# Another beginning for block 0, the next block's elimination and part of the activation on VectorE, and later stores

## The chip, the cores and the metric

The kernel runs on one core of a Trainium2 chip. Its engines have queues of their own: TensorE (PE; PEld is its weight load), VectorE (DVE), ScalarE (ACT), GpSimd (POOL), and SyncE (SP), which here issues all the DMAs. Each engine works through its queue in order and waits on semaphores for the others. The metric is the device time of one execution in microseconds: 2344.46 us is the median of three runs (2343.63 to 2352.79).

## The reference

Three stages follow each other. Shapes: batch 4, heads 8, sequence 768, head size 48; 3072 tokens of 384 columns; a hidden layer of 2048; 8 experts with 1024 hidden columns each.

```
k_n = k / (norm(k) + 1e-6)
for t in range(768):                       # delta rule, one state per (batch, head)
    y[t]  = q[t] @ state
    state = state + beta[t] * outer(k_n[t], v[t] - state.T @ k_n[t])
x = y as (tokens, 384)
h = x @ w_in                               # 384 -> 2048
g = h * tanh(softplus(h))                  # "Mish"
x = g @ w_out                              # 2048 -> 384
P = exp(x @ w_gate - max)                  # (3072, 8)
8 times: P /= row sums; P /= column sums; P *= 3072 / 8
out = sum over e of P[:, e] * (relu(x @ w1[e]) @ w2[e])
```

All inputs are fp32, except that w_in and w_out reach the kernel as 64-bit words whose bits it turns into fp32 itself.

## The kernel before

**Blocks.** The sequence is cut into six blocks of 128 steps (two chunks of 64), so a block has 512 tokens. The main loop goes through the blocks. In one block it does the hidden layer of 2048 in 16 units (`s0` to `s15`, then four marks `f1` to `f4` without a first product), and then expert 0 in 8 units (`s16` to `s23`). A unit is 128 hidden columns: nine products into a PSUM bank of 512 columns (`gemm1`, L296), the activation, and the second product. Each fp32 operand is split into a rounded high part and a remainder (`xh`, `xl`; `gh`, `gl`; two halves of `w`), and three products are added up. After the loop the experts 1 to 7 are done by another code, which the change does not touch.

**The delta rule of the next block** is laid beside a block's units. For each block, `st_g` multiplies keys with keys and queries, VectorE masks the results (`gx`), two or three transpositions bring them into `lane`, and 30 pairs of small operations (`elim_ops`, L784 and L790) invert the triangular diagonal blocks: a product, then an addition, each waiting for the one before. `st_lane_out` transposes back into `t11` and `yd`. `st_m1` and `st_m2` join the half blocks by products (copies at L815 and L607), `st_place` puts the diagonal blocks back. Then a chain of 16 stages follows, four kinds (`st_z`, `st_w`, `st_s`, `st_y`) for two chunks and two batch pairs, each reading what the one before wrote through VectorE.

`window(c)` says at which mark of block c each step stands: `PLACES` gives per block the mark of `st_lane_out`, the marks of the chain, of the square sums, mask products, `st_g`, operand loads and the start of the elimination. Elimination steps wait in a list `eq`, from which `fill(us)` and `tick` (after each VectorE operation made through `vec`) take as many as their costs allow.

**Block 0** has nothing in front of it, so its own delta rule is the beginning of the kernel: loads, `st_gk` and norms, elimination, joining, chain, transposition into `x1h`, `x1l` (`st_x1`), then the first unit. In it TensorE is given fillers: `warm(n)` is n products of 512 zero columns into a spare bank, and `run_warm(cols, ...)` puts some behind each stage. During the beginning and block 0 the weights are also decoded: `begin_decode` scales the high words on ScalarE (L202), three VectorE operations (L185, L188, L193) put the words together, and `convert` rounds the high part on ScalarE (L248), subtracts on GpSimd (L249), and stores the result in DRAM (`wd`, L253), so that later blocks load it with one DMA (L242). The buffers of the words are reused, so that a decode four chunks on waits for a conversion; some are the key and query tiles of block 0.

The activation of block 0 is `m_a` (Mish from PSUM into `mi_x` in SBUF), `m_c` (copy to `gh`, L977, and the remainder `gl` on GpSimd, L978). `y0_done` and `x2_done` copy results into `xr` and issue its store right there (L959, L1002). In the last block `g_load` prepares the next experts' weights and at once fetches the following ones.

Of the kernel before, what the change touches and what calls it, by code (L numbers as in the profile page):

```python
# [84 lines left out]
def delta_mish_sinkhorn_kernel(  # L85
# [144 lines left out]

    def convert():
# [190 lines left out]
    def g_load():  # L422
# [19 lines left out]
        g_fetch()  # L442
# [84 lines left out]
    if True:  # L527
# [173 lines left out]


# [18 lines left out]
        def st_gq(c, t):  # L721
# [46 lines left out]
        def lane_in_ops(c):  # L768
# [5 lines left out]
            )  # L774

# [89 lines left out]
        def first_r(c, t):  # L865
            rt[c, t] = r_p.tile([128, DM], F32, tag="r", name="r")
            nc.scalar.activation(out=rt[c, t], in_=vt(c)[:, t, :], func=AF.Copy, scale=-1.0)
# [75 lines left out]
        y0ps = {}  # L943

# [7 lines left out]
        def y0_done(c):  # L952
# [6 lines left out]
            nc.sync.dma_start(out=y0_dram[c], in_=y)  # L959
# [10 lines left out]
        def m_a(u):  # L970
            nc.scalar.activation(out=mi_x[u % 2], in_=hps.pop(u), func=AF.Mish)

        def m_c(u):
            p = mi_x[u % 2]
# [3 lines left out]
            nc.gpsimd.tensor_tensor(out=l, in0=p, in1=h.bitcast(F32), op=ALU.subtract)  # L978
# [14 lines left out]
        def x2_done(c):  # L993
# [8 lines left out]
            nc.sync.dma_start(out=x2_dram[c], in_=xr)  # L1002
# [31 lines left out]
        with tc.manual_schedule():  # L1034
# [8 lines left out]
            for t in range(4):  # L1043
                load_part(0, t, 1)
            for t in range(4):
                load_kq(1, t)
            load_vt(0)
            for n in range(4):
                fetch(n)
            load_vt(1)  # L1050
            nc.sync.dma_start(out=id_sb, in_=ident)
# [19 lines left out]
            for op in root_ops(0) + norm_ops(0, ALL):  # L1071
                op()
            for t in range(4):
                prep_mb(0, t, (nc.vector, nc.gpsimd)[t % 2])
                g0[t]()
            for _, op in lane_in_ops(0):
                op()
# [5 lines left out]

            for t in range(4):
                prep_ss(1, t)
            prep_root(1)
            nc.scalar.activation(out=mi_s[0][:, 0:1], in_=seed_sb, func=AF.Mish)
# [4 lines left out]
            el(12)  # L1092
            for op in root_ops(1) + norm_ops(1, ALL):
                el(1)
                op()
            for t in range(4):
                prep_mb(1, t, nc.gpsimd)
            for t in range(2):
                mask_p(0, t)
            for t in range(2):  # L1100
                prep_v(0, t)
                first_r(0, t)
            for t in range(4):
                mask_g(1, t, nc.gpsimd)
            for t in range(2, 4):
                prep_v(0, t)
                mask_p(0, t)
            for n in range(3):
                begin_decode(n)
            el(len(e0) - 16)  # L1110
# [4 lines left out]
            in1 = deque(op for _, op in lane_in_ops(1))  # L1115
            in1.popleft()()
            elim_eng = [nc.gpsimd]
            ops1 = deque(op for _, op in elim_ops(1, elim_eng))

            def elim1(n, eng):  # L1120
                elim_eng[0] = eng
                for _ in range(min(n, len(ops1))):
                    ops1.popleft()()

            run_warm(2048, lambda: st_m1(0, 0), lambda: st_m1(0, 1))
            st_place(0, 0, (0, 2))
            while in1:
                in1.popleft()()
            run_warm(2048, lambda: st_m2(0, 0))

            def step(pool, decode, make, dve):
                elim1(pool, nc.gpsimd)
                decodes(decode)
                elim1(dve, nc.vector)
                converts(make)

            step(8, 1, 0, 0)
            run_warm(1536, lambda: st_w(0, 0), lambda: st_w(0, 1))
            st_place(0, 1, (0, 2))
            run_warm(1280, lambda: st_m2(0, 1))  # L1140
            step(8, 2, 1, 0)
            run_warm(1024, lambda: st_s(0, 0), lambda: st_s(0, 1))
            run_warm(1024, lambda: st_y(0, 0), lambda: st_y(0, 1))
            for n in range(4, 6):
                fetch(n)
            begin_decode(3)
            step(4, 3, 2, 0)
            run_warm(1024, lambda: st_z(0, 2), lambda: st_z(0, 3))
            step(4, 4, 2, 8)
            run_warm(512, lambda: st_w(0, 2), lambda: st_w(0, 3))  # L1150
            begins(6)
            step(2, 5, 3, 0)
            run_warm(512, lambda: st_y(0, 2), lambda: st_y(0, 3))
            for n in range(6, 8):
                fetch(n)
            step(4, 6, 5, 6)
            converts(4)
# [17 lines left out]
        def drain_decode():  # L1175
            decodes(U1)
            converts(U1)

        PLACES = [
            (5, spread(5 + 3, 26, 2, 16), 21 - 5,  # L1180
             [21 - 2, 21 - 1, 21, 21 + 1], spread(21, 27, 2, 8), 18, 26, 24),
            (3, spread(3 + 3, 19, 1, 16), 8 - 5,
             [8 - 2, 8 - 1, 8 + 1, 8 + 3], spread(8, 19, 1, 8), 1, 27, 19),
# [284 lines left out]
```

## Time and profile before

| what | value |
|---|---|
| median of three runs | 2344.46 us |
| profiled execution | 2351.13 us, span 2349.4 us |
| TensorE busy | 2262.2 us, 96% of the span |
| VectorE, ScalarE, GpSimd busy | 1239.3, 619.7, 527.3 us |
| mean granted TensorE clock | 0.968 of full speed |
| first product of a unit (L296) | 864 of 419 ns and 432 of 409 ns |
| elimination of block 0 ends, first unit starts, block 1 starts | 59.9, 111.5, 275.4 us |
| block 2, 3, 4, 5 start; end of the loop | 428.6, 570.4, 711.6, 838.1, about 954 us |

A granted clock of 1.00 is 2.4 GHz and 0.50 is 1.2 GHz; between them stands a mean over a stretch. The page's slices show VectorE at eight to nine tenths only in the first 180 us, and TensorE near nine tenths behind that. A row of the profile names a line, an engine, an operation, the written and read tiles and their shapes.

### The profile page before, as it was taken

To read this page: it belongs to the slowest core of one execution; us is meant where nothing else is said; L and a number is where in the kernel's file an instruction comes from. 1 tells how busy PE (TensorE), PEld (TensorE's weight loads), DVE (VectorE), ACT (ScalarE), POOL (GpSimd) and SP (SyncE) were. 2 spreads that over 40 slices of the span, in tenths; PEclk is the share of its full clock that TensorE was granted. 3 is DMA by queue.
4 is the path that set the end of the run, shared out by engine and by line. 5 is a ranking of instruction groups with operands and counts; after the bars stand their busy time and mean duration, and the time that the engine had idled before them with its cause. 6 is when DMAs were issued, how large, how long until landed. Compare 5 with 4: busy or idle time off the path is not lost.

```text
span 2349.4 us, 41970 instructions
## 1 busy us (share of the span) xinstructions
PE 2262.2 (96%) x18012; PEld 2090.3 (89%) x18012; DVE 1239.3 (53%) x2009; ACT 619.7 (26%) x1012; POOL 527.3 (22%) x439
## 2 busy tenths in 40 slices
PE   8688999999999999999999999999999999999998
PEld 4477777878788887899999999999999999999998
DVE  8884724518153112776554555555555555545554
ACT  5244332333223233222211221131122122112111
POOL 5586442241411133131300110030020002002000
PEclk6799989999999999999999999999999999999999
DMA  6357643636444455432332132231223113221321
GB/s 174 122 202 214 200 151 127 213 122 202 158 158 162 162 215 215 166 119 93 122 135 81 55 121 81 82 127 49 81 81 135 65 71 121 81 81 68 108 87 48
DMA packets 74441, 297.04 MB, mean 126 GB/s; under 512 B 7504, under 2 KB 39504, under 8 KB 68880
## 3 DMA queue, kind: packets, MB, share of 16 engines
q1 hardware_dynamic: 74256, 294.36, 36.3%
q8 instruction: 142, 2.33, 0.4%
q14 instruction: 43, 0.35, 0.0%
HBM read 247.15 MB, written 47.19 MB: 125 GB/s over the span
## 4 chain that ended last, share of the span: by engine, by line
PE 51%; issue 30%; DVE 7%; DMA 5%; POOL 5%; SPq 1%; ACT 1%; POOLq 0%; DVEq 0%; ACTq 0%
PE psh L296 12%; PE o L1347 11%; PE b L487 10%; PE x L989 8%; PE y L318 3%; DMA gr<-in_w_dram 3%; POOL gw L439 2%; DVE t L784 1%; DVE lane L790 1%; DMA w<-wd 1%; POOL gx L439 1%; PE psa L739 1%; PE psa L878 1%; PE psa L912 1%; DVE lane L772 1%
## 5 line engine op out<-in xcount | busy, mean ns | idle before, releaser
L487 PE MATMUL b<-gx,gw 128*128 128x256 f32 x3564 | 448.7, 283 | 6.4 <-DVE gate L363 2.5
L487 PEld LDWEIGHTS b<-gx,gw 128*128 128x128 f32 x3564 | 441.3, 191 | 10.1 <-ACT gt L509 3.7
L1347 PE MATMUL o<-gw,gh 128*128 128x384 f32 x1728 | 440.4, 335 | 2.0 <-DVE acc L1352 2.0
L514 ACT ACTIVATE gh<-gt 128x1024 fp32r<-128x1024 f32 x168 | 178.3, 1061 | 620.3 <-DVE gt L513 620.3
L296 PE MATMUL psh<-xh,w 128*128 128x512 f32 x864 | 291.4, 419 | 20.8 <-DMA w<-wd 11.6
L1347 PEld LDWEIGHTS o<-gw,gh 128*128 128x128 f32 x1728 | 307.6, 189 | 2.5 <-issue 2.5
L515 DVE SCALAR_TENSOR_TENSOR gl<-gt,gh 128x1024 fp32r<-128x1024 f32 x168 | 207.7, 1236 | 189.4 <-ACT gh L514 189.4
L1347 PE MATMUL o<-gw,gl 128*128 128x384 f32 x864 | 289.7, 335 | 0.0
L510 DVE TENSOR_TENSOR gt<-b,gt 128x512 f32<-128x512 f32 x168 | 116.2, 691 | 309.6 <-PE b L487 245.3
L1347 PE MATMUL o<-gx,gh 128*128 128x384 f32 x960 | 247.5, 339 | 2.4 <-DVE acc L1352 2.4
L487 PE MATMUL b<-gx,gx 128*128 128x256 f32 x1980 | 244.3, 280 | 2.0 <-ACT gt L509 1.0
L487 PEld LDWEIGHTS b<-gx,gx 128*128 128x128 f32 x1980 | 240.5, 188 | 3.8 <-ACT gt L509 1.7
L978 POOL TENSOR_TENSOR gl<-x,gh 128x512 fp32r<-128x512 f32 x96 | 128.0, 1333 | 405.7 <-ACT gh L977 397.2
L439 POOL TENSOR_TENSOR gw<-gr,gw 128x512 fp32r<-128x512 f32 x72 | 90.8, 1294 | 567.5 <-ACT gw L437 567.5
L296 PEld LDWEIGHTS psh<-xh,w 128*128 128x128 f32 x864 | 162.1, 197 | 62.6 <-issue 17.1
L296 PE MATMUL psh<-xl,w 128*128 128x512 f32 x432 | 176.6, 409 | 3.9 <-DVE xl L607 3.9
L1347 PEld LDWEIGHTS o<-gx,gh 128*128 128x128 f32 x960 | 171.6, 188 | 2.9 <-issue 2.0
L1347 PEld LDWEIGHTS o<-gw,gl 128*128 128x128 f32 x864 | 162.4, 188 | 0.4
L1347 PE MATMUL o<-gx,gl 128*128 128x384 f32 x480 | 162.6, 339 | 0.0
L509 ACT ACTIVATE gt<-b 128x256 f32<-128x256 f32 x168 | 63.8, 380 | 349.8 <-PE b L487 328.9
L989 PE MATMUL x<-gh,w 128*128 128x512 f32 x576 | 151.4, 399 | 0.0
L439 POOL TENSOR_TENSOR gx<-gr,gx 128x512 fp32r<-128x512 f32 x40 | 51.3, 1312 | 436.0 <-ACT gx L437 436.0
(182 smaller groups left out, 3026.0 us busy)
## 6 DMA issues: line engine op xcount, KB each, us to landing
w<-wd SPq DMA_DIRECT2D x120, 768.0 KB, 4.5
gx<-xcd SPq DMA_DIRECT2D x36, 2304.0 KB, 9.0
gr<-in_w_dram SPq DMA_DIRECT2D x56, 384.0 KB, 3.7
wd<-w SPq DMA_DIRECT2D x24, 768.0 KB, 4.4
xcd<-gx SPq DMA_DIRECT2D x6, 2304.0 KB, 11.6
kq<-in_qkb_dram SPq DMA_DIRECT2D x20, 256.0 KB, 6.7
vt<-in_vtok_dram SPq DMA_DIRECT2D x6, 768.0 KB, 8.6
kq<-in_w_in_dram SPq DMA_DIRECT2D x12, 384.0 KB, 4.6
```

Source lines behind the costliest of these rows:

```text
L296: mm(ps, lhsT=wi(u, pw, kc), rhs=(xh, xl)[px][:, kc, :], start=(n == 0), stop=(n == 3 * KD - 1))
L318: mm(o[t], lhsT=(h, l)[ph][:, t * 128:(t + 1) * 128], rhs=wo(u, pw, 0, DM), start=(f == 0 and n == 0), stop=(f == U2 - 1 and n == 2))
L439: nc.gpsimd.tensor_tensor(out=w[:, 1, q:q + 512], in0=r[:, q:q + 512], in1=w[:, 0, q:q + 512].bitcast(F32), op=ALU.subtract)
L487: mm(ps, lhsT=w[:, pw, a * 128:a * 128 + 128], rhs=x[:, px, b, :], start=(n == 0), stop=(n == last))
L509: nc.scalar.activation(out=t[:, 7], in_=b0[:, 0], func=AF.Copy)
L510: tt(out=t[:, 0:7:6], in0=b1, in1=t[:, 7:8].to_broadcast([128, 2, 256]), op=ALU.add)
L514: nc.scalar.activation(out=h, in_=t[:, 0:4], func=AF.Relu)
L515: nc.vector.scalar_tensor_tensor(out=l, in0=t[:, 0:4], scalar=0.0, in1=h.bitcast(F32), op0=ALU.max, op1=ALU.subtract)
L739: mm(ps[0:64, :, i], lhsT=k[64:64 + D, 0, h, :], rhs=k[64:64 + D, 0:2, h, :], start=True, stop=True)
L978: nc.gpsimd.tensor_tensor(out=l, in0=p, in1=h.bitcast(F32), op=ALU.subtract)
L989: mm(x2ps[c][k], lhsT=wo(u, pw, k * 128, k * 128 + 128), rhs=(h, l)[pg], start=(f == 0 and n == 0), stop=(f == U1 - 1 and n == 2))
L1347: mm(o[t], lhsT=(h, l)[ph][:, z, (t % 2) * 128:(t % 2) * 128 + 128], rhs=w[:, pw, at:at + DM], start=(g == 0 and fi == 0 and n == 0), stop ...
```

## The change

**The beginning.** `diag_left` copies, on ScalarE, the second diagonal block of each product beside the first, so that `lane_in_one` needs one transposition; GpSimd clears the copies behind it. The scalings of v in block 0 go to ScalarE (`prep_v_act`, and `first_r` with the scale `minus_ne`). The products with the queries stay in four PSUM banks, and VectorE masks them later, between the chain's results. The mask products and maskings of block 1 come after block 0's elimination instead of beside it. The load of v of block 0 goes ahead of block 1's operands. `run_warm` becomes `run`, with single fillers left. The decode scalings of four chunks stand behind ScalarE's copies of products; four chunks are converted before the loop, the fifth is only begun.

**Block 0.** Mish is written in place into its PSUM bank for the 16 units, and VectorE computes the remainder. Of block 1's elimination GpSimd does 18 steps, VectorE takes the others from `eq`, three or so per unit (`fill(1.2)`). `PLACES` puts block 1's `st_lane_out` at mark 11 instead of 5, and its chain two by two at marks 14 to 22 instead of 8 to 15; the products for block 2 stand two marks later, the loads of their operands where they stood.

**Stores.** The store of a converted chunk is issued after the next conversion's fetch, the stores of `xr` at unit 4 and at the third unit of expert 0. In the last block a fetch for expert 1 stands two marks behind the `g_load` that frees its buffer.

```diff
+    late_stores = deque()
+    def flush_stores():
+        while late_stores:
+            late_stores.popleft()()
...
         if kind(i) == "again":
+            flush_stores()
             nc.sync.dma_start(out=w.bitcast(F32), in_=w_dram[ch])
...
-        if ch in w_dram:
-            nc.sync.dma_start(out=w_dram[ch], in_=w.bitcast(F32))
...
+        flush_stores()
+        if ch in w_dram:
+            late_stores.append(lambda: nc.sync.dma_start(out=w_dram[ch], in_=w.bitcast(F32)))
...
             def post():
-                raw(k[0:64, 1], ps[0:64])
-                raw(k[64:128, 2], ps[64:128])
+                for p, o in ((0, k[0:64, 1]), (64, k[64:128, 2])):
+                    if masked:
+                        nc.vector.tensor_tensor(
+                            out=o, in0=ps[p:p + 64],
+                            in1=mask_sb[p:p + 64, None, :].to_broadcast([64, H, CH]), op=ALU.mult,
+                        )
+                    else:
+                        raw(o, ps[p:p + 64])
...
+        def diag_left(c, t):
+            g = gx(c)[:, t]
+            for p in (32, 96):
+                nc.scalar.activation(out=g[p:p + 32, :, 0:32], in_=g[p:p + 32, :, 32:64], func=AF.Copy)
+        def lane_in_one(c):
+            v = gx(c).rearrange("p t h x -> p x (t h)")
+            return [
+                (1.94, lambda: nc.vector.transpose(out=lane, in_=v[:, 0:32, :])),
...
         def m_a(u):
-            nc.scalar.activation(out=mi_x[u % 2], in_=hps.pop(u), func=AF.Mish)
+            if u < U1:
+                nc.scalar.activation(out=hps[u], in_=hps[u], func=AF.Mish)
...
         def m_c(u):
-            p = mi_x[u % 2]
+            p = hps.pop(u) if u < U1 else mi_x[u % 2]
...
-            nc.gpsimd.tensor_tensor(out=l, in0=p, in1=h.bitcast(F32), op=ALU.subtract)
+            eng = nc.vector if u < U1 else nc.gpsimd
+            eng.tensor_tensor(out=l, in0=p, in1=h.bitcast(F32), op=ALU.subtract)
...
-            nc.sync.dma_start(out=y0_dram[c], in_=y)
+            late_xr.append(lambda: nc.sync.dma_start(out=y0_dram[c], in_=y))
...
-            run_warm(1024, *[lambda t=t: st_gq(0, t) for t in range(3)])
-            run_warm(1024, lambda: st_gq(0, 3))
+            gq = [st_gq(0, t, True) for t in range(4)]
             for t in range(4):
-                run_warm(512, *[lambda hf=hf: st_g(1, t, hf, False) for hf in range(2)])
...
-            (5, spread(5 + 3, 26, 2, 16), 21 - 5,
...
+            (11, two(14, 15, 17, 18, 19, 20, 21, 22), 16, [21, 22, 23, 24], two(23, 24, 25, 26), 18, 26, 26),
...
-                    if not c and f < m0:
-                        elim1(10, nc.gpsimd)
+                    if f == 4:
+                        flush_xr()
...
-                    fill(2.0)
+                    fill(2.0 if c else 1.2)
...
+                    if f == U1 + 2:
+                        flush_xr()
```

**Three places in the queues.** In the rows below, `bits` and `kq` are words being decoded, `lane` and `t` belong to the elimination, `us` to the chain, `xl` and `gl` are remainders, `psa` and `psh` are PSUM banks.

VectorE before, where the first unit's operands are made (the last elimination steps of the beginning, the low parts `xl`, chain results):

```order
L784 TENSOR_TENSOR t_169<-lane 128x198 [waits DVE_49]
L790 TENSOR_TENSOR lane<-lane,t_169 128x9x22 [waits DVE_49]
L607 TENSOR_TENSOR xl_1208<-psa,xh_1207 128x512 [waits Activation_49] x3
L607 TENSOR_TENSOR us_164<-psa,us_165 48x384 [waits PE_49]
L607 TENSOR_TENSOR us_164<-psa,us_165 48x384
L607 TENSOR_TENSOR us_166<-psa,us_167 48x384 [waits PE_49]
L607 TENSOR_TENSOR us_166<-psa,us_167 48x384
```

VectorE after, at the same place:

```order
L185 TENSOR_SCALAR bits_177<-bits_177 128x768 [waits DMAHW7_49,DMAHW6_49]
L188 SCALAR_TENSOR_TENSOR bits_177<-bits_177 128x768 [waits DVE_49]
L193 SCALAR_TENSOR_TENSOR bits_177<-bits_177 128x768 [waits DVE_49]
L824 TENSOR_TENSOR t_169<-lane 128x210 [waits Pool_49]
L830 TENSOR_TENSOR lane<-lane,t_169 128x21x10 [waits DVE_49]
L824 TENSOR_TENSOR t_169<-lane 128x220 [waits DVE_49]
L617 TENSOR_TENSOR xl_1152<-psa,xh_1151 128x512 [waits Activation_49] x3
L1031 TENSOR_TENSOR gl<-psh,gh 128x512 [waits Activation_49]
```

Ahead of `xl` three elimination steps now stand whose first waits for GpSimd, and the first remainder `gl` of block 0 comes behind it.

VectorE before, in the middle of block 0's units (decode steps and the joining of block 1):

```order
L185 TENSOR_SCALAR kq_142<-kq_142 128x768 [waits DMAHW7_49,DMAHW0_49]
L188 SCALAR_TENSOR_TENSOR kq_142<-kq_142 128x768 [waits DVE_49,Activation_49]
L193 SCALAR_TENSOR_TENSOR kq_142<-kq_142 128x768 [waits DVE_49]
L607 COPY mb_179<-psa 32x512 [waits PE_49]
L607 COPY mb_179<-psa 32x512
L185 TENSOR_SCALAR kq_143<-kq_143 128x768 [waits DMAHW5_49,DMAHW4_49,Pool_49]
L188 SCALAR_TENSOR_TENSOR kq_143<-kq_143 128x768 [waits DVE_49,Activation_49]
L193 SCALAR_TENSOR_TENSOR kq_143<-kq_143 128x768 [waits DVE_49]
```

VectorE after, in the middle of block 0's units:

```order
L1031 TENSOR_TENSOR gl<-psh,gh 128x512 [waits PE_49,Activation_49]
L824 TENSOR_TENSOR t_169<-lane 128x228
L830 TENSOR_TENSOR lane<-lane,t_169 128x12x19 [waits DVE_49]
L824 TENSOR_TENSOR t_169<-lane 128x220 [waits DVE_49]
L185 TENSOR_SCALAR kq_145<-kq_145 128x768 [waits DMAHW5_49,DMAHW4_49]
L188 SCALAR_TENSOR_TENSOR kq_145<-kq_145 128x768 [waits DVE_49]
L193 SCALAR_TENSOR_TENSOR kq_145<-kq_145 128x768 [waits DVE_49]
L1031 TENSOR_TENSOR gl<-psh,gh 128x512 [waits PE_49,Activation_49]
```

Between two remainders there are now three or four elimination steps and one decode; the joining has moved to later units.

SyncE before, at the end of block 0 and the start of block 1 (weight loads `w`, the store `y0d`, the operands `kq`):

```order
L242 DMA w_88<-wd_93 128x1536 [waits DMAHW3_49,PE_49]
L959 DMA y0d_73<-xr 128x1536 [waits DMAHW4_49,DVE_49,Activation_49]
L617 DMA kq_146<-in_qka_dram 48x1024 [waits DMAHW5_49]
L618 DMA kq_146<-in_qkb_dram 64x2x512 [waits DMAHW6_49]
L617 DMA kq_147<-in_qka_dram 48x1024 [waits DMAHW7_49]
L618 DMA kq_147<-in_qkb_dram 64x2x512 [waits DMAHW0_49]
L617 DMA kq_148<-in_qka_dram 48x1024 [waits DMAHW1_49]
L618 DMA kq_148<-in_qkb_dram 64x2x512 [waits DMAHW2_49]
L617 DMA kq_149<-in_qka_dram 48x1024 [waits DMAHW3_49]
L618 DMA kq_149<-in_qkb_dram 64x2x512 [waits DMAHW4_49]
L242 DMA w_89<-wd_94 128x1536 [waits DMAHW5_49,PE_49]
L242 DMA w_1209<-wd_95 128x1536 [waits DMAHW6_49,PE_49]
```

SyncE after, at the same place, from the last operands on:

```order
L628 DMA kq_148<-in_qkb_dram 64x2x512 [waits DMAHW1_49]
L627 DMA kq_149<-in_qka_dram 48x1024 [waits DMAHW2_49]
L628 DMA kq_149<-in_qkb_dram 64x2x512 [waits DMAHW3_49]
L250 DMA w_89<-wd_94 128x1536 [waits DMAHW4_49,PE_49]
L250 DMA w_1153<-wd_95 128x1536 [waits DMAHW5_49,PE_49]
L250 DMA w_85<-wd_96 128x1536 [waits DMAHW6_49,PE_49]
L1008 DMA y0d_73<-xr 128x1536 [waits DMAHW7_49,DVE_49,Activation_49]
L250 DMA w_86<-wd_97 128x1536 [waits DMAHW0_49,PE_49]
```

The store stands behind three more weight loads; the operands of block 3 still stand ahead of these.

## Rows read from the trace of the kernel before

**Rows 1.** Windows: stretch, length, busy time (instructions) per engine, granted clock, DMA share, GB/s.

```profile
0.00:111.45 111.45, 85.04 (x1125) 54.89 (x1125) 96.90 (x149) 44.26 (x133) 61.95 (x66) 0.69 0.46 141
122.24:202.78 80.54, 73.69 (x934) 60.63 (x930) 67.41 (x61) 39.80 (x58) 64.02 (x44) 0.96 0.61 206
202.78:275.44 72.66, 64.77 (x443) 55.18 (x439) 33.50 (x70) 25.25 (x48) 40.45 (x35) 0.91 0.70 222
838.06:954.40 116.34, 110.91 (x503) 92.66 (x502) 33.80 (x80) 38.69 (x60) 41.04 (x31) 0.96 0.52 192
```

**Rows 2.** TensorE waits, start: who for whom, total us, times, longest.

```profile
PE psa L826 <- DVE t L799: 7.1, 1, 7.1
PE psa L912 <- DVE us L607: 6.5, 1, 6.5
PE psh L296 <- DVE xl L607: 3.9, 1, 3.9
```

**Rows 3.** VectorE timeline: start, us, engine, line, operation, tiles, shapes, idle before.

```profile
17.35 3.89 DVE L772 STREAM_TRANSPOSE lane<-gx 32x1024 f32<-32x1024 f32 x2
37.44 1.35 DVE L784 TENSOR_TENSOR t<-lane 128x240 f32<-128x240 f32 x1
59.89 2.01 DVE L799 STREAM_TRANSPOSE t<-lane 128x1024 f32<-128x1024 f32 x1
75.78 0.96 DVE L193 SCALAR_TENSOR_TENSOR xr<-xr 128x768 int32<-128x768 int32 x1
```

**Rows 4.** VectorE groups, 260 to 290 us: count, busy us, mean ns, idle before.

```profile
L790 DVE TENSOR_TENSOR lane<-lane,t 128x30 f32<-128x30 f32 (+14 forms) x30 | 11.6, 387 | 0.8
L784 DVE TENSOR_TENSOR t<-lane 128x30 f32<-128x30 f32 (+14 forms) x30 | 11.5, 382 | 0.9
L311 DVE SCALAR_TENSOR_TENSOR hl<-psh,hh 128x512 fp32r<-128x512 f32 x4 | 2.7, 682 | 0.0
```

**Rows 5.** Windows: products with fillers; block 0’s elimination beside GpSimd.

```profile
16.75:48.00 31.25, 31.25 (x272) 21.24 (x272) 29.96 (x54) 21.15 (x98) 15.86 (x14) 0.50 0.73 219
28.40:44.90 16.50, 16.50 (x119) 11.62 (x118) 16.02 (x15) 8.15 (x22) 15.83 (x13) 0.50 0.74 264
```

**Rows 6.** TensorE groups, 57 to 111 us: fillers between the joining stages.

```profile
L1022 PE MATMUL spare<-f 128*128 128x512 f16 (+1 forms) x41 | 14.9, 468 | 0.0
```

**Rows 7.** GpSimd groups, 73 to 98 us: elimination of block 1.

```profile
L790 POOL TENSOR_TENSOR lane<-lane,t 128x30 f32<-128x30 f32 (+11 forms) x12 | 8.9, 738 | 0.9
```

**Rows 8.** TensorE groups, 428 to 571 us: one chain operation.

```profile
L878 PE MATMUL psa<-r,gx 64*64 64x48 f32 x128 | 4.5, 220 | 0.0
```

**Rows 9.** VectorE groups, 117 to 200 us: decoding in block 0.

```profile
L193 DVE SCALAR_TENSOR_TENSOR kq<-kq 128x768 int32<-128x768 int32 x10 | 17.8, 1782 | 0.3
L188 DVE SCALAR_TENSOR_TENSOR kq<-kq 128x768 int32<-128x768 int32 x10 | 16.4, 1640 | 3.7 <-ACT kq L202 2.8
L185 DVE TENSOR_SCALAR kq<-kq 128x768 int32<-128x768 int32 x10 | 10.3, 1027 | 0.1
```

**Rows 10.** GpSimd groups, 117 to 200 us: the activation’s remainder.

```profile
L978 POOL TENSOR_TENSOR gl<-x,gh 128x512 fp32r<-128x512 f32 x13 | 20.9, 1608 | 3.2 <-ACT gh L977 2.5 <-DMA wd<-w 0.6
```

**Rows 11.** TensorE waits in block 0 after its first unit.

```profile
PE psa L739 <- issue: 5.5, 1, 5.5
```

**Rows 12.** TensorE waits in block 1, and clock behind the wait.

```profile
PE psh L296 <- DMA w<-wd: 6.7, 1, 6.7
290.00:310.00 20.00, 13.27 (x151) 10.62 (x151) 8.53 (x12) 5.34 (x11) 7.83 (x3) 0.57 0.63 200
```

**Rows 13.** SyncE timeline, beginning of block 1.

```profile
281.85 0.32 SPq L959 DMA_DIRECT2D y0d<-xr  x1
287.39 3.72 SPq L242 DMA_DIRECT2D w<-wd  x4
```

**Rows 14.** TensorE waits in blocks 2 and 3.

```profile
PE psa L861 <- issue: 2.7, 1, 2.7
```

**Rows 15.** TensorE waits in blocks 4 and 5.

```profile
PE psh L296 <- DMA w<-wd: 4.9, 3, 2.1
```

More of the change, by code (lines that the diff above doesn't have):

```diff
@@ L700, in prep_v, with prep_v_act @@
             prep_scale(c, t, vt(c), nrms[c % 2][1])
+        def prep_v_act(c, t):
+            ne = nrms[c % 2][1]
+            for h in range(H):
+                x = vt(c)[:, t, h * D:h * D + D]
+                nc.scalar.activation(out=x, in_=x, func=AF.Copy, scale=ne[:, t * H + h:t * H + h + 1])
         def raw(out, in_):
@@ L866, in first_r @@
             rt[c, t] = r_p.tile([128, DM], F32, tag="r", name="r")
-            nc.scalar.activation(out=rt[c, t], in_=vt(c)[:, t, :], func=AF.Copy, scale=-1.0)
+            for h in range(H):
+                hs = slice(h * D, h * D + D)
+                nc.scalar.activation(
+                    out=rt[c, t][:, hs], in_=vt(c)[:, t, hs], func=AF.Copy, scale=minus_ne[:, t * H + h:t * H + h + 1]
+                )
         def st_w(c, t):
@@ L1114, in delta_mish_sinkhorn_kernel, with work @@
             st_lane_out(0)
[L1115 to L1116 removed]
+            for op in norm_ops(1, ALL):
+                op()
+            for t in range(4):
+                prep_mb(1, t, nc.gpsimd)
+            for t in range(4):
+                mask_g(1, t, nc.gpsimd)
+            def work(decode, make):
+                decodes(decode)
+                converts(make)
+            run(lambda: st_m1(0, 0), lambda: st_m1(0, 1))
+            st_place(0, 0, (0, 2))
+            run(lambda: st_m2(0, 0))
+            st_place(0, 1, (0, 2))
+            run(lambda: st_m2(0, 1))
+            warm(1)
+            work(1, 1)
+            run(lambda: st_w(0, 0), lambda: st_w(0, 1))
+            gq[0]()
+            gq[1]()
+            for t in range(2, 4):
+                prep_v_act(0, t)
+            for t in range(4):
+                diag_left(1, t)
+            warm(1)
+            run(lambda: st_s(0, 0), lambda: st_s(0, 1))
+            in1 = [op for _, op in lane_in_one(1)]
             elim_eng = [nc.gpsimd]
[L1118 removed]
+            ops1 = deque(elim_ops(1, elim_eng))
             def elim1(n, eng):
@@ L1122, in elim1 @@
                 for _ in range(min(n, len(ops1))):
[L1123 to L1143, printed above, removed]
+                    ops1.popleft()[1]()
+            run(lambda: st_y(0, 0), lambda: st_y(0, 1))
+            for op in in1:
+                op()
             for n in range(4, 6):
                 fetch(n)
[L1146 to L1153, printed above, removed]
+            work(2, 2)
+            elim1(8, nc.gpsimd)
+            warm(1)
+            run(lambda: st_z(0, 2), lambda: st_z(0, 3))
+            gq[2]()
+            gq[3]()
+            work(3, 3)
+            warm(1)
+            run(lambda: st_w(0, 2), lambda: st_w(0, 3))
+            elim1(10, nc.gpsimd)
+            work(4, 4)
+            warm(1)
+            run(lambda: st_y(0, 2), lambda: st_y(0, 3))
             for n in range(6, 8):
                 fetch(n)
-            step(4, 6, 5, 6)
-            converts(4)
+            begins(5)
+            elim_eng[0] = nc.vector
+            eq.extend(ops1)
             early_ctx.close()
```

76 lines of the change are left out of this document (41 added, 35 removed).

## The prediction

> **What bounds the kernel now.** I read the busy time by stretch first, then who TensorE waits for in each stretch, and then VectorE's, GpSimd's and SyncE's own rows at those waits. From block 1 on TensorE is busy nearly all the time; what can be won lies in its waits, in the clock it loses behind them, and in the 111.45 us before the first weight product, in which TensorE is 85.04 us busy, much of it with fillers, at a mean granted clock of 0.69 [rows 1]. There VectorE (96.90 us busy) is the engine that the others wait for: TensorE waits 7.1 us for the end of block 0's elimination (L799), 6.5 us for a chain result behind decode steps, and 3.9 us for the low part of block 0's activations [rows 2]. In block 0 the first thirteen units after the opening one take 80.54 us and hold 73.69 us of TensorE, the rest of the block 72.66 us with 64.77 us [rows 1]. Blocks 1 to 5 show a few waits for weights and for "issue" [rows 12, 14, 15]. The gated experts behind them keep their code and are taken as unchanged.
>
> **The beginning up to the joining.** Two ScalarE copies per tile put the second diagonal blocks beside the first, so that one transposition does what three did: the pair at L772, 3.89 us, goes [rows 3]. In its place come one small VectorE negation and, behind the last product, two ScalarE copies. Neither is in the trace; they cost between nothing and the 1.4 us of two 0.68 us operations on 512 columns [rows 4]. I take 1.0, as the copies are half as wide. The elimination then starts near 18.3 us instead of 21.2 (17.35 + 3.89).
>
> The elimination ran from 21.2 to 59.89, 38.7 us [rows 3]. Between 28.4 and 44.9 GpSimd was busy 15.83 of 16.5 us, and a 240-column product took 1.35 us there [rows 3, 5]. Block 2's elimination, with GpSimd mostly idle, shows the same 60 operations at 387 and 382 ns, 23.1 us and 1.7 of gaps [rows 4]. The change takes masks, scalings and the mask multiplications out of this stretch, so I use 25 us: the first back transposition (2.0 us) ends at 45.3 instead of 61.9. The bounds are 24 and 31, if the one power operation and two clears left on GpSimd cost half of what its work costs now.
>
> TensorE must be there too. Its products kept it busy 31.25 us of 31.25 from 16.75 on, at 1.2 GHz, granted 0.50, fillers included [rows 5]. Sixteen fillers at 0.468 us [rows 6] go, so the products end near 40.5, and twelve fillers that stay end near 46.1. The joining begins at 46 against 61.9: 15.9 us less. That the clock stayed at its lower level under a full queue with fillers tells me that losing these fillers loses nothing there.
>
> **The joining.** It held 41 fillers, 14.9 us; nine stay, so 11.6 us leave TensorE's queue [rows 6]. Against that, the sixteen operations of the joining cost 1.13 us each at 2.4 GHz (4.5 over four) [rows 8], 18 us. At the mean clock of this stretch, 0.69, they are 26, at 0.50 they are 36. Some of the 10 us lies beside VectorE, which is late anyhow; I charge 6. The wait of 6.5 us holds decode and elimination steps of which one decode stays: I count 3, a gain of 3.5 [rows 2]. The products with the queries are now masked on VectorE out of PSUM, eight operations at 0.68, 5.5 us, between a result and the next [rows 4]. And a new wait: at the opening unit three elimination steps stand on VectorE ahead of the low parts of the activations, and they wait for GpSimd, which has 18 steps at 0.74 (13.3 us) [rows 7] and two weight subtractions, each at most 2.4 us by L978's 1.6 for two thirds of the columns [rows 10], behind the lane transposition. That is 18 us against about 17 for the chain beside it, plus decode waits of about 3: 4 us of waiting where 3.9 stood, so nothing. The sum is -11.6 + 6 - 3.5 + 5.5 = -3.6. Two decodes and 14 eliminations less stand on VectorE here, which could add 3. I take -4, between -8 and +6. The beginning together gives -20 us.
>
> **Block 0.** Two things move to VectorE: the remainder of each activation (L978, 20.9 us for thirteen on GpSimd [rows 10]) at 0.68 from PSUM, 8.8 us [rows 4], and 39 of the 42 elimination steps that GpSimd does not take, 15 us. Two more decodes come at about 2.5 us (0.6 + 2 x 0.96 undisturbed [rows 3]), 5 us. Away go the chain's results, about 11 us, now placed behind. VectorE's 67.4 us [rows 1] become 85. Part of the 67.4 is disturbance: ten decodes cost 44.5 us, 4.45 each, instead of 25 [rows 9], some 24 us with the other disturbed copies. GpSimd's 64.0 us fall by about 21 + 6 and grow by 4, to 42, so I keep two thirds of the 24 and get 77 to 78 us for the thirteen units. This is also TensorE's time: the activation now stays in its PSUM bank until VectorE has read it, and the product two units later needs that bank, so TensorE follows VectorE's queue, at about 5.9 us a unit. 80.5 becomes 78.
>
> The second stretch takes the whole chain of block 1: about 16 operations at 1.13, 18 us, where a quarter stood, +13.8. It fills the places behind the first GEMM, where 5.5 us of waiting stood (the operand's load moves two marks away from its product) [rows 11] and some 4 us went to a granted clock of 0.91 [rows 1]. In exchange each chain result now waits for the one before it, about 4.4 us. 72.7 becomes about 80.6. Block 0 gives +5, between -10 and +20.
>
> **Blocks 1 to 5.** At the start of block 1 SyncE holds the store of y0 until 281.85, and the weight loads are issued at 287.39 [rows 13]; TensorE waits 6.7 us for them, and over the next stretch the clock is 0.57, so that 13.27 busy us did the work of about 7.5 [rows 12]. With the store three units later, the loads go out as their slots come free. I count -6.7, -6 for the clock, and -1.3 for the chain spread over four more marks: -14, between -6 and -17. In blocks 2 and 3 the "issue" wait (2.7 us and its like) [rows 14] falls when stores, loads and operands are issued in one burst; pulling them apart is worth -3, between -8 and +3. In block 5 the next expert's fetch stood ahead of the weight loads and waited for GpSimd: 4.9 us in three waits [rows 15], and a clock of 0.96 over 116 us, of which I count 3: -8, between -3 and -10.
>
> **Sum.** -20 + 5 - 14 - 3 - 8 = -40. The profiled execution took 2351.13 us (span 2349.4, 1.7 around it), so it would take 2311; the median of the runs is 6.7 lower, and -40 on 2344.46 gives 2304.
>
> **Rivals.**
> A. VectorE loses all of GpSimd's time. The 1.35 us product [rows 3] was slowed by the full measure; the decodes, with 4.45 for 2.5, by less. If nearly all of GpSimd's 42 us block VectorE, save some 10 beside operations that read PSUM, the thirteen units take 61 + 32 = 93: +15, 2319.
> The Trainium skill, "SBUF — State Buffer", section on SBUF's two separate sides, says that VectorE and GpSimd take a shared port pair as an exclusive lock for a whole instruction, and that a VectorE operation with two SBUF inputs is among those that want it. By that rule the moved eliminations are the worst kind of work to put beside GpSimd, which speaks for A; the trace agrees at 1.35 us, less so at the decodes.
>
> B. The lighter GpSimd frees VectorE more than I grant, and units run at 5 us: -12, 2292. For it: undisturbed the unit is 2.5 + 3 x 0.38 + 0.68 = 4.3.
>
> C. The late stores do only half of what they should, since eight operand loads still stand ahead of the weights in block 1 and the last fetch still waits in block 5: +13, 2317. A and C together come to 2332.
>
> D. Slower: VectorE's queue in block 0. If decodes keep their 4.45 us, the three steps beside them cost 1.35 each and the remainder 0.68, a unit takes 9.2 us and the thirteen 119 instead of 78: +41. TensorE then idles half of each unit, and the second stretch begins at the lower clock, as behind the 6.7 us wait [rows 12], some +14: 2359. From 9.1 us a unit on, all other gains are gone. Against it: GpSimd has a third less to do.
>
> **Numbers.** Forecast 0.47, A 0.18, B 0.14, C 0.11, A with C 0.05, D 0.05. What a measurement of this kernel can tell from no change is about 0.5%, 11.7 us, so faster means under 2332.7 and slower over 2356.2: 0.88 faster (the four cases, less 0.02 for their edges), 0.07 the same, 0.05 slower. The forecast's own range is 2288 to 2320; with B below and A with C above, 2277 to 2330.
>
> **What would show it.** The first back transposition of block 0 should start near 43 us, without a product of over 1 us before it; the first weight product's opening unit should end about 20 us earlier, at a clock of 0.5 in between. In block 0 the first products of a unit should be released by VectorE's remainder, at 5 to 6.5 us a unit: over 9 is D, about 4.5 is B. In blocks 1 and 5 no wait for weights should be left. The forecast is wrong if the joining takes as much longer without fillers as the elimination is shorter, or if the second stretch of block 0 passes 90 us.

## The result: 2326.65 us, half of the gain that was forecast

| | before | after |
|---|---|---|
| median | 2346.81 us (4 runs) | 2326.65 us (2323.18 to 2327.35, 4 runs) |
| profiled execution | 2351.13 us | 2327.31 us, span 2325.5 us |
| TensorE, VectorE, ScalarE, GpSimd busy | 2262.2, 1239.3, 619.7, 527.3 us | 2241.0, 1245.8, 626.4, 474.4 us |
| granted clock | 0.968 | 0.973 |

The ratio is 0.9915, 95% interval 0.9896 to 0.9934: 20 us less where 40 were forecast, and outside the forecast's own range of 2288 to 2320. The spans differ by 23.9 us; before's profiled run lay 4 us above its median. I read the profile as the forecast was built, by stretch: where each block begins, and who TensorE waits for in it.

Windows of the kernel after (stretch, length, busy time of TensorE, weight load, VectorE, ScalarE, GpSimd with instructions, clock, DMA share, GB/s): the beginning to the first unit, units 1 to 13 of block 0, its second stretch, block 1, blocks 2 to 4, block 5.

```profile
0.00:89.73 89.73, 66.35 (x1077) 52.99 (x1077) 72.60 (x138) 50.41 (x168) 43.10 (x46) 0.70 0.58 176
95.79:178.65 82.86, 65.33 (x549) 50.47 (x546) 80.78 (x98) 39.20 (x59) 36.22 (x23) 0.94 0.65 219
178.65:265.67 87.02, 79.44 (x826) 69.67 (x823) 45.54 (x77) 25.81 (x50) 41.88 (x35) 0.88 0.56 197
265.67:416.22 150.55, 142.13 (x1391) 118.86 (x1390) 82.63 (x175) 44.06 (x82) 45.16 (x41) 0.94 0.48 157
416.22:824.36 408.14, 401.52 (x3976) 334.18 (x3974) 153.96 (x300) 123.92 (x226) 110.60 (x98) 0.98 0.51 165
824.36:930.25 105.89, 105.34 (x503) 89.46 (x502) 33.14 (x80) 38.62 (x60) 40.86 (x31) 1.00 0.60 210
```

They answer to [rows 1]; block 1 and blocks 2 to 4 of the kernel before are these two windows:

```profile
275.44:428.55 153.11, 143.35 (x1391) 119.48 (x1390) 72.57 (x157) 44.18 (x82) 45.30 (x41) 0.92 0.48 156
428.55:838.06 409.51, 402.26 (x3976) 334.68 (x3974) 153.98 (x300) 123.81 (x226) 110.41 (x98) 0.98 0.49 164
```

| stretch | forecast | measured |
|---|---|---|
| beginning, to unit 1 (122.24 to 95.79) | -20 | -26.4 |
| units 1 to 13 of block 0 (80.54 to 82.86) | -2.5 | +2.3 |
| second stretch of block 0 (72.66 to 87.02) | +7.9 | +14.4 |
| block 1 | -14 | -2.6 |
| blocks 2 to 4 | -3 | -1.4 |
| block 5 (116.34 to 105.89) | -8 | -10.4 |
| sum | -40 | -24.1 |

The beginning and block 5 gave more than forecast; block 0 and block 1 together lost 23 us against it.

**The beginning.** VectorE's timeline (start, us, line, operation), against [rows 3]: one transposition, undisturbed steps, the first back transposition at 40.33 instead of 59.89.

```profile
29.34 0.41 DVE L824 TENSOR_TENSOR t<-lane 128x240 f32<-128x240 f32 x1
40.33 2.08 DVE L839 STREAM_TRANSPOSE t<-lane 128x1024 f32<-128x1024 f32 x1
```

The elimination took 22 us (18.4 to 40.3), where I had put 25. TensorE's products and fillers ahead of the joining, which I had put at 46.1, ended at 40.2, with the clock there at 0.74 instead of 0.50 [rows 5]. The opening unit took 6.1 us instead of 10.8.

```profile
16.75:42.56 25.81, 17.55 (x206) 14.96 (x201) 23.68 (x65) 23.25 (x110) 7.39 (x3) 0.74 0.84 248
89.73:95.79 6.06, 5.63 (x73) 4.01 (x73) 2.68 (x5) 2.55 (x5) 0.00 (x0) 0.72 0.01 3
```

**Block 0.** TensorE's waits from unit 1 to the end of block 0 (who for whom, total us, times, longest):

```profile
PE psh L305 <- DVE gl L1031: 17.5, 10, 3.0
PE psa L922 <- DVE r L617: 3.7, 1, 3.7
PE psa L956 <- DVE us L617: 2.9, 1, 2.9
```

As foretold, a unit's first product waits for the remainder on VectorE, at 6.4 us a unit in the mean. Why VectorE is late shows in one unit of its timeline, and in GpSimd's beside it:

```profile
123.13 0.68 DVE L1031 TENSOR_TENSOR gl<-psh,gh 128x512 fp32r<-128x512 f32 x1
123.73 0.38 DVE L830 TENSOR_TENSOR lane<-lane,t 128x220 f32<-128x220 f32 x1
124.14 0.38 DVE L824 TENSOR_TENSOR t<-lane 128x210 f32<-128x210 f32 x1
124.55 1.93 DVE L830 TENSOR_TENSOR lane<-lane,t 128x210 f32<-128x210 f32 x1
```

```profile
124.22 2.03 POOL L257 TENSOR_TENSOR w<-kq,w 128x768 fp32r<-128x768 f32 x1 [3.42 <-ACT w L256]
```

The third step takes 1.93 us instead of 0.38 and ends 0.2 us after GpSimd's weight subtraction (126.25). L257 follows the decode by the 0.9 us of ScalarE's rounding, so in eight of the units it meets an elimination step; in the later ones, and with GpSimd's scalings and masks behind it, it meets decode steps and copies. Taken against the shortest time of the same operation and shape in the kernels before, after and of the first experiment, VectorE's steps in these thirteen units took about 24 us too long, an estimate from the timelines; in the kernel before it was about 23.

**The second stretch.** The copies that put block 1's diagonal back, on VectorE, ahead of the chain's first result:

```profile
176.38 7.71 DVE L851 COPY gx<-yd 32x512 f32<-32x512 f32 x4
184.11 1.38 DVE L617 COPY gx<-psa 32x512 f32<-32x512 f32 x2
186.13 1.01 DVE L617 TENSOR_TENSOR r<-psa,vt 128x384 f32<-128x384 f32 x2
```

From 176.75 to 187.1 GpSimd runs four weight subtractions and two mask products without a gap, and the four copies take 1.9 us in the mean (0.42 to 3.2). TensorE waits 3.7 us for `r`, and then, as behind the second wait (203.10 to 206.03), works at the lower clock:

```profile
186.73:193.50 6.77, 6.77 (x72) 6.00 (x73) 3.23 (x6) 0.00 (x0) 0.38 (x1) 0.50 1.01 346
206.03:216.50 10.47, 10.45 (x166) 9.71 (x167) 5.91 (x11) 1.22 (x2) 7.51 (x3) 0.55 0.02 4
```

At 0.50 and 0.55 the two windows lose 3.4 and 4.7 us, somewhat more than the waits themselves (6.6).

**Block 1.** The weights are there: no wait for them, against 6.7 us in [rows 12]; the loads stand ahead of the store now, against [rows 13]. But TensorE waits 4.6 us for the elimination, and its clock falls behind that:

```profile
PE psa L866 <- DVE t L839: 4.6, 1, 4.6
```

```profile
292.08:305.80 13.72, 9.14 (x155) 7.83 (x156) 8.98 (x17) 4.44 (x8) 1.29 (x1) 0.75 0.17 58
```

VectorE began that elimination at 253.33 and ended it at 296.5. The change had moved block 3's norms two marks ahead in block 1, so that they now stand inside the elimination, and VectorE stood still for 1.4 us of it waiting for GpSimd's power operation:

```profile
253.33 2.04 DVE L793 STREAM_TRANSPOSE lane<-gx 128x1024 f32<-128x1024 f32 x1
283.69 1.23 DVE L688 TENSOR_SCALAR ne<-ne 128x32 f32<-128x32 f32 x1 [1.44 <-POOL ne L666]
294.50 2.01 DVE L839 STREAM_TRANSPOSE t<-lane 128x1024 f32<-128x1024 f32 x1
```

In the kernel before, the same transposition ended at 291.89, while TensorE waited for weights until 296.85:

```profile
289.86 2.03 DVE L799 STREAM_TRANSPOSE t<-lane 128x1024 f32<-128x1024 f32 x1
296.85 1.19 PE L296 MATMUL psh<-xh,w 128*128 128x512 f32 x2 [6.73 <-DMA w<-wd]
```

**Blocks 2 to 4.** The waits for "issue" that the change was to shorten stayed, 4.7 us before (two lines) and 4.1 after:

```profile
PE psa L861 <- issue: 2.9, 2, 2.7
PE psa L860 <- issue: 1.8, 1, 1.8
PE psa L880 <- issue: 4.1, 2, 2.3
```

### The profile page after: what moved, and what is told of

It reads as the page before. It is cut to its first block, busy times and chain, and to the rows that moved or that the text cites. A ratio compares the mean times of both kernels' runs of the same rounds, so it can differ in the third digit from the quotient of the medians.

```text
span 2325.5 us, 41900 instructions
## 1 busy us (share of the span) xinstructions
PE 2241.0 (96%) x17964; PEld 2087.5 (90%) x17964; DVE 1245.8 (54%) x2054; ACT 626.4 (27%) x1049; POOL 474.4 (20%) x388
## 4 chain that ended last, share of the span: by engine, by line
PE 58%; issue 25%; DVE 8%; POOL 4%; DMA 4%; ACT 1%; SPq 0%; DVEq 0%; POOLq 0%; ACTq 0%
PE o L1409 15%; PE b L497 14%; PE psh L305 11%; PE x L1042 7%; PE y L327 4%; DMA gr<-in_w_dram 3%; POOL gw L448 2%; POOL gx L448 1%; PE psa L761 1%; DVE lane L830 1%; PE psa L956 1%; PE psa L922 1%; DVE t L824 1%; PE psa L900 1%; PE psa L1061 1%
## 5 line engine op out<-in xcount | busy, mean ns | idle before, releaser
L1031 POOL TENSOR_TENSOR gl<-x,gh 128x512 fp32r<-128x512 f32 x80 | 103.0, 1288 | 377.6 <-ACT gh L1029 376.8
```

Source lines behind the costliest of these rows:

```text
L1031: eng.tensor_tensor(out=l, in0=p, in1=h.bitcast(F32), op=ALU.subtract)
```

## The experiments

My theory after this: (1) in block 0 GpSimd's subtractions hold VectorE; (2) in block 1 the elimination is next in line behind the weights; (3) each wait of TensorE costs itself and about as much again in clock. The rivals: VectorE merely has too many instructions, and the chain's small products lower the clock wherever they stand. The changes are against the kernel after, but for `e4_stores_only`; the ratios are to the kernel before, as the 0.9915 of the kernel after is.

**The weight subtraction on VectorE** (`e1_wsub_dve`).

```
-        nc.gpsimd.tensor_tensor(out=w[:, 1], ...
+        (nc.vector if kind(i) == "wide" and i >= 4 else nc.gpsimd).tensor_tensor(out=w[:, 1], ...
```

> The changed kernel, but the weight subtraction of chunks 4 to 15 (L257, 2.0 us on GpSimd, one a unit of block 0) runs on VectorE. Theory, VectorE waits for GpSimd: in most units of block 0 one elimination step takes 1.9 instead of 0.38 us while L257 runs on GpSimd, and TensorE follows VectorE. Without L257 on GpSimd a unit is 2.5 (decode) + 0.68 + 3 x 0.38 + 0.96 = 5.3 us instead of 6.4; twelve units, -13 us: 2314, with no elimination step over 0.5 us beside an L257. Rival, VectorE simply has too many instructions there: 12 x 0.96 more, +11 us: 2338, units at 7.3 us.

2314.21 us (2310.02 to 2316.02), ratio 0.9865 (0.9832 to 0.9899). Windows of the units 1 to 13 and of the second stretch, and two of VectorE's groups in the units:

```profile
96.10:169.22 73.12, 62.47 (x549) 48.51 (x545) 70.94 (x112) 40.90 (x59) 4.14 (x3) 0.98 0.73 253
169.22:247.89 78.67, 74.81 (x826) 65.59 (x823) 40.70 (x75) 25.15 (x49) 38.38 (x33) 0.93 0.64 214
```

```profile
L257 DVE TENSOR_TENSOR w<-kq,w 128x768 fp32r<-128x768 f32 x9 | 8.6, 951 | 0.0
L824 DVE TENSOR_TENSOR t<-lane 128x240 f32<-128x240 f32 (+14 forms) x15 | 4.9, 329 | 0.4
```

VectorE got twelve more instructions and was done sooner: the thirteen units fell from 82.86 to 73.12 us, most of them to about 5.1, with no prolonged elimination or decode step. GpSimd's own work fell from 36.2 to 4.1 us, since the scalings and six masks then stood ahead of this stretch in its queue; the edit tells "GpSimd beside VectorE" from "too many instructions", and not L257 from the masks.

The Trainium skill, "SBUF — State Buffer", section on SBUF's two separate sides, says that a VectorE operation with two SBUF inputs and a GpSimd operation that reads SBUF exclude each other for a whole instruction. The 1.93 beside the 2.03 us agrees. GpSimd's power operation, whose inputs are SBUF tiles too, does not: 5.50 us from 25.17, and VectorE's steps beside it stayed at 0.39 to 0.41.

```profile
25.17 5.50 POOL L666 TENSOR_TENSOR ne<-ss,half_sb 128x32 f32<-128x32 f32 x1 [4.81 <-ACT sq L660]
```

**Block 1 two marks later** (`e2_b1_later`). In this kernel the masks of block 3 are written before the joining has read its own tiles; the instructions are the same.

```
-            (5, spread(8, 23, 1, 16), ...
+            (7, spread(10, 25, 1, 16), ...
```

> The changed kernel, but in block 1 the drain of block 2's elimination and all that follows it stands two marks later (5 becomes 7, the chain 8..23 becomes 10..25). Theory, behind the weights the elimination was next in line in block 1: the wait of 4.58 us before L866 goes, and with it the granted clock of 0.75 over 13.7 us (3.4 us): -8, 2319. Rival, the chain's small products lower the clock and wait wherever they stand: only the wait changes its place, 2325 to 2329.

2317.33 us (2310.87 to 2321.73). Block 1:

```profile
266.36:406.78 140.42, 135.87 (x1392) 113.46 (x1390) 83.85 (x175) 43.92 (x82) 45.64 (x41) 0.99 0.50 169
```

The wait before L866 is gone, and the longest that is left is 2.1 us. Ten us less: 3.9 of them idle time of TensorE (8.4 to 4.55), the rest its clock (0.94 to 0.99). In the three later kernels in which this edit leaves the masks intact, block 1 took 142.6 to 142.8 us, so that about eight of the ten are borne out. They are most of the 11.4 us of the forecast's 14 that had not come.

**Chain stages out of f2 to f4** (`e3_chain_out_of_f`). Here the masks of two tiles of block 2 are overwritten before their use.

```
-  ... two(14, 15, 17, 18, 19, 20, 21, 22) ...
+  ... two(14, 15, 20, 21, 22, 23, 24, 25) ...
```

> The changed kernel, but in block 0 no chain stage stands at f2 to f4 (marks 17 to 19, between the two GEMM stretches); the six of them go, two by two, beside the expert's units s19 to s21 and the rest moves up. Theory, the stages packed where no weight products stand cost the second stretch its clock and its waits: the unit with f1 to f4 falls from 23.5 to about 12 us, the later units rise by 6 x 1.13 = 7: -5, 2322, and the second stretch falls from 87.0 to about 82. Rival, the gap between the GEMMs waits for its operand anyway (5.5 us in the kernel before): it comes back with a lower clock, second stretch 87 to 92, 2327 to 2332.

2332.51 us (2326.16 to 2337.26, 10 runs), second stretch 90.83: my theory of this run fell. (The six stages went to marks 20 to 22, which are s16 to s18 and not s19 to s21.) The rival's figures came, but not its cause: no product of TensorE waited for a load in this stretch. The wait before the fourth pair grew from 2.9 to 9.8 us:

```profile
PE psa L956 <- DVE us L617: 9.8, 1, 9.8
```

```profile
212.58 1.77 DVE L688 TENSOR_SCALAR ne<-ne 128x32 f32<-128x32 f32 x1 [5.55 <-POOL ne L666]
215.22 2.28 DVE L617 TENSOR_TENSOR us<-psa,us 48x384 f32<-48x384 f32 x4
```

With the marks empty, the norms of block 2 came too soon: VectorE waited in L688 for GpSimd's power operation, and the chain's result stood behind it.

**The late stores alone** (`e4_stores_only`), on the kernel before:

```
-            nc.sync.dma_start(out=y0_dram[c], in_=y)
+            late_xr.append(lambda: nc.sync.dma_start(out=y0_dram[c], in_=y))
...
+                        rest[MARKS[f + 2]].append(g_fetch)
```

> The kernel before with the late stores alone (y0, x2 and weight stores behind the next loads, the next fetch two marks later in block 5); the beginning, the fillers, the order by marks and the activation are those of before. The forecast's terms: block 1 -12.7 (6.7 wait, 6 clock), blocks 2 and 3 -3, block 5 -8: -24, 2323. Rival, behind the weights the elimination is next in line: it ended at 291.8 where the first joining product would now be due at about 290, so 2 us of waiting and part of the lower clock come back: block 1 -7, in all -18, 2329.

2331.95 us (2321.59 to 2337.29, 10 runs), ratio 0.9945 (0.9926 to 0.9965), some 12 us less than the kernel before in the same series (2343.57). The profiled executions differ by 25 us, since this one lay 6 us below its median and that of before above, so the stretches below show where the late stores act rather than what they are worth in the median. By the profile block 5 gives 10.5, as after the whole change, and block 1 only 8.2 of 12.7 (153.11 to 144.90):

```profile
273.80:418.70 144.90, 137.24 (x1391) 114.77 (x1390) 72.97 (x157) 44.18 (x82) 45.32 (x41) 0.98 0.49 165
```

VectorE's back transposition, and TensorE's joining behind it:

```profile
288.22 2.25 DVE L809 STREAM_TRANSPOSE t<-lane 128x1024 f32<-128x1024 f32 x1
```

```profile
290.62 2.06 PE L836 MATMUL psa<-t,gx 32*32 32x32 f32 x119
295.62 0.43 PE L836 MATMUL psa<-t,gx 32*32 32x32 f32 x9 [2.94 <-issue]
```

For block 1 the rival's figure is about right and its cause isn't: the elimination was ready at 290.47, and the joining began at 290.62, without a wait but with nothing to spare. The 2.9 us stand in the midst of the joining's products, which waited for their issue, as in [rows 14]; I did not find what holds that up.

**Both edits together** (`e5_both`: the first, and the second with masks and operands of block 3 moved along).

> The changed kernel with both edits that paid: the weight subtraction of chunks 4 to 15 on VectorE, and in block 1 the drain of the elimination, the chain, the masks and the operands of block 3 two marks later. Theory, the two losses are separate (VectorE waits for GpSimd in block 0; the elimination is next in line in block 1): block 0 from its unit 1 on 152 us as in the kernel with the subtraction moved, block 1 140 to 141 us; 2314 - 10 = 2304. Rival, the faster block 0 brings block 1 to the elimination as much earlier and the wait comes back: 2312.

2307.45 us (2306.40 to 2310.39), block 0 from its unit 1 on 155.1, block 1 142.7: the two losses add, to within the 3 us by which the forecast was missed.

**Block 1's diagonal put back by ScalarE** (`e6_place_act`).

```
-  ... st_place(nxt, hf, (0, 2)) ...
+  ... st_place(nxt, hf, (0, 2) if nxt > 1 else range(4)) ...
```

> The changed kernel, but in block 0 the copies that put block 1's diagonal back (L851, four on VectorE, 7.7 us at 176.4) run on ScalarE with the other four. Theory, these copies are held up by three weight subtractions on GpSimd beside them, the chain's first result waits behind them, and the 3.7 us wait before L922 with the lower clock behind it (0.50 for 6.8 us, worth 3.4) hangs on them: wait and clock go, second stretch of block 0 from 87 to 80, 2320. Rival, the first result waits for the joining's own products and ScalarE is late with the eight copies instead: 2325 to 2329, the wait stays at 3 to 4 us.

2321.98 us (2317.63 to 2324.07). The wait before L922 is gone; the second stretch fell by 3.8 to 83.18, not by 7, because a wait further down the chain took its place:

```profile
PE psa L940 <- DVE us L617: 4.2, 2, 3.9
```

**The third pair at f1** (`e7_s_at_f1`: 17 becomes 16 in the list of marks).

> The changed kernel, but the third pair of chain stages of block 0 stands at f1 instead of f2, ahead of the split of the GEMM's result. Theory, the wait of 2.94 us before L956 and the clock of 0.50 from 207.2 to 216.5 behind it (4.7 us) come from the pair's results standing on VectorE behind the split (3 x 0.63 + 0.68): both go, -7, 2320; the first wait of 3.7 us stays. Rival, the chain's small products keep the clock down by themselves in f1 to f4, wait or not: only the wait goes, -3, 2324.

2327.70 us: nothing gained. The wait before L956 went, and 4.4 us before L940 came, behind L688 once more:

```profile
209.89 1.77 DVE L688 TENSOR_SCALAR ne<-ne 128x32 f32<-128x32 f32 x1 [4.02 <-POOL ne L666]
```

**All four** (`e8_all`).

> All four edits together on the changed kernel: weight subtraction of chunks 4 to 15 on VectorE, block 1 two marks later, block 1's diagonal put back by ScalarE, the chain's third pair at f1. Theory, each wait of TensorE costs itself and about as much again in clock, and the edits take three of them away: 2304 - 7 = 2297. Rival, ScalarE, with eight copies and the activations, becomes late in block 0: 2304 to 2310.

2303.22 us (2299.40 to 2304.48), ratio 0.9811 (0.9793 to 0.9830), six us more than my theory, with 4.4 us before L940 in place of the other waits of the second stretch.

**Norms three marks earlier** (`e9_norm_early`: all four, and `16` becomes `13` in block 0's places).

> The kernel with the four edits, and block 2's norms three marks earlier in block 0 (the power operation on GpSimd at s14, the steps behind it on VectorE at f1). Theory: with the third pair at f1 the wait went on to L940 (4.36 us), because VectorE held the chain's results behind a norm step (L688) that waits 5.4 us for GpSimd's power operation; with the norms early that wait goes and its clock with it, second stretch of block 0 from 77.7 to about 70: 2303 - 8 = 2295. Rival, the wait goes on again to the next result on VectorE, as it did three times: 2300 to 2304.

2302.11 us (2296.84 to 2303.64), ratio 0.9807 (0.9768 to 0.9846). In the profile the second stretch, 77.70 us with the four edits, has lost its waits but for 1.1 us, and has the full clock:

```profile
169.75:241.80 72.05, 70.76 (x826) 61.63 (x823) 37.16 (x70) 24.85 (x48) 40.38 (x35) 1.00 0.70 238
```

So the stretch holds 70.8 us of work at 2.4 GHz, the whole chain included: the chain's small products do not lower the clock by themselves. The time of the whole kernel, within the rival's range, can't tell this run from the last.

**Block 1's chain in pairs** (`e10_b1_pairs`).

> The same, and block 1's chain in pairs from s10 to f1 with the last two stages at f2 and f3, so that only stages whose results ScalarE takes stand between the two GEMM stretches. Theory, waits come from VectorE's results between the stretches (2.1 us before f2's stages in block 1): the wait and some clock go, -3: 2292. Rival, two stages beside one unit wait for each other: block 1 longer by 1 to 3 us, 2296.

2303.12 us (2296.72 to 2307.64); block 1 took 139.6 instead of 142.6 us, but a 2.1 us wait stayed, before L761 now. No gain that can be told.

**Fillers back in the joining** (`e11_fillers`: `run` becomes `run_warm(1024, ...)`, nine times).

> The changed kernel with two fillers of 512 columns behind every chain stage of the joining again (36 more). Forecast: fillers only stand in TensorE's queue and the clock there doesn't follow them: 36 x 0.28 us at the joining's mean clock, 10 us, of which 4 to 6 lie beside VectorE: 2331 to 2333, joining from 47 to 52 us. Rival 1, TensorE waits for VectorE there anyway: 2327. Rival 2, the granted clock, 0.57 in the changed kernel's joining and 0.74 with the fillers of before, goes up, and the stages get shorter by more than the fillers cost: 2320, joining 41 us.

2327.17 us (2322.70 to 2328.98). The joining of the kernel after, and of this one:

```profile
42.56:89.73 47.17, 34.82 (x661) 29.58 (x661) 39.77 (x51) 18.53 (x43) 29.73 (x32) 0.57 0.35 119
```

```profile
42.56:90.70 48.14, 38.66 (x694) 25.91 (x694) 39.12 (x53) 18.47 (x43) 29.72 (x32) 0.79 0.35 117
```

The clock follows the fillers, from 0.57 to 0.79, as rival 2 had it, and the time stays, as rival 1 had it: the joining is 1.0 us longer. TensorE's busy time grows by 3.8 us and its idle time shrinks by 2.9; the higher clock pays for part of the fillers, the waits for the rest.

**The remainder back on GpSimd** (`e12_rem_pool`).

```
-            eng = nc.vector if u < U1 else nc.gpsimd
+            eng = nc.gpsimd
...
```

In the part cut away, `m_a` writes `mi_x` in SBUF again.

> The changed kernel with block 0's activation through SBUF again and its remainder (L1031) on GpSimd. Theory, what counts in block 0 is how long GpSimd's subtractions hold VectorE: one more of 1.3 to 1.6 us a unit holds it longer than the 0.68 us that VectorE is spared, units at about 7: block 0 from its unit 1 on +8, 2335. Rival, VectorE's own queue is what counts: 13 x 0.68 less, 2318.

2327.55 us (2321.20 to 2329.28), between the two. The windows show why:

```profile
95.34:184.06 88.72, 73.34 (x549) 55.14 (x545) 85.93 (x87) 40.20 (x59) 59.02 (x36) 0.87 0.60 205
184.06:265.16 81.10, 77.23 (x827) 67.69 (x823) 37.95 (x71) 25.23 (x49) 44.76 (x38) 0.89 0.62 211
```

The units are slower by 5.9 us, as the theory has it; the second stretch is shorter by as much, since the diagonal's copies met less of GpSimd (three at 0.42 us and one at 1.99, 3.3 us instead of 7.7) and the 3.7 us wait did not come. In sum the activation in PSUM, with its remainder on VectorE, is worth nothing that can be told here.

## Why the forecast was half right

- **Beginning, -20, measured -26.4.** Right that VectorE's elimination sets its time. The joining begins at 42.6 instead of 61.9, 19 us earlier and not 15.9, because the elimination took 3 us less than my 25 and TensorE's products were done earlier than I had them. Wrong is how the joining's -4 was put together. I had -11.6 for the fillers and +6 for the lower clock; the run with fillers gives both together 1.0 us. The joining is 2.4 us shorter, and the opening unit, in which I had expected as long a wait as before, 4.7.
- **Units of block 0, -2.5, measured +2.3: a step that failed.** Right that TensorE follows VectorE's queue. But "so I keep two thirds of the 24", 16 us of VectorE's disturbance, because GpSimd had a third less to do [rows 9, 10]: about 24 us of it were left, though GpSimd's work fell further than I had put it, from 64.0 to 36.2 us. With 4.1 us of it, in the first experiment, under 2 us were left. So the disturbance does come from GpSimd, but goes by which step stands beside its 2 us and not by its share. Rival A named this; its 93 us are too high, since GpSimd did 36 us and not its 42. B and D are out at 6.4 us a unit.
- **Second stretch, 80.6, measured 87.0: a step that failed.** The terms I wrote come to 81.4 (13.8 - 5.5 - 4 + 4.4 is 8.7, not 7.9). "In exchange each chain result now waits for the one before it, about 4.4 us", and four us of clock were to come back. The waits in all were 7.6 us, close to before's 7.9; the work is 70.8 us at the full clock, as the run with the early norms shows, so that 87.0 - 7.6 - 70.8 = 8.6 us went to the clock. I had priced the wait that went away with its clock, and the waits that I added without.
- **Block 1, -14, measured -2.6: the largest failure.** "I count -6.7, -6 for the clock": the wait for weights went as described, so rival C is out, and I did not ask who ends next. In the kernel before, the elimination was ready at 291.89, hidden by the weights that came at 296.85; with the late stores alone it is just in time; and the change moves it later (`eq0` from 24 to 26, the norms ahead of it). Two marks more for it gave 8 to 10 us back.
- **Blocks 2 to 4, -3, measured -1.4: the step has no support.** The -3 was for the "issue" wait [rows 14], and that stayed, 4.1 us against 4.7. The -1.4 can't be told from nothing: in kernels whose edits leave these blocks alone they took 407 to 411 us. What holds the issue up is open.
- **Block 5, -8, measured -10.4.** Right: the waits for weights [rows 15] are gone, and the late stores alone give the same 10.5.

The misses partly cancel: block 0 and block 1 lost 23 us against the forecast, the beginning and block 5 gave 9 more than it.

Four edits that take waits away reach 2303.22 us. That this is the forecast's 2304 is chance: one of them takes GpSimd's subtractions out of block 0, which the forecast had not counted on.

## What to carry to other kernels

When a wait goes, price it by the next thing in line: read when that ends, from the trace, before counting the whole wait as gained. Price every wait that a change adds on TensorE with its clock, if the old one was priced so; in block 0 that was about twice its length. Count not how busy GpSimd is but which VectorE operation stands beside each of its long ones, and put no result that TensorE needs behind a step that waits for GpSimd.

## What the runs showed of the hardware that I had not expected

- VectorE's short two-input steps last as long as the rest of GpSimd's subtraction (1.93 against 0.38 us), but neither the 5.50 us power operation nor two clears of 1 us each in the beginning prolonged any of them.
- That power operation takes 5.50 us for 32 columns; a product on 30 columns took GpSimd 0.25 us (L824 at 73.59).
- Whether a wait of some 2 us costs the clock varies. These are two like units of the kernel after, in blocks 2 and 3, with the two waits for issue, 1.8 and 2.3 us:

```profile
424.82:434.53 9.71, 7.95 (x183) 6.43 (x179) 6.42 (x10) 7.17 (x13) 5.45 (x2) 1.00 0.44 149
563.45:576.46 13.01, 10.68 (x184) 8.47 (x178) 6.42 (x10) 7.15 (x13) 7.94 (x3) 0.74 0.34 111
```

The second unit is 3.3 us longer, and only 0.6 of it is the wait. That this makes blocks 2 to 4 differ by up to 4 us between the kernels is likely and not shown.
